# Three batch-1 projections with the weights as the moving operand, in four column tiles

## The chip, the cores and the metric

The program runs on one core of one Trainium2 chip. The metric is the time in device microseconds. One more execution was taken with the hardware profiler; its rows are what this document reads. Engines are named as the profile does: PE is TensorE's matmul, PEld its weight load, DVE is VectorE, ACT ScalarE, POOL GpSimd, SP the queue that issues the DMAs.

## The reference

Eight rows (batch 8, one token each, 448 wide) go through four layers: attention, a feed-forward layer, the same attention again, the same feed-forward again. The second attention reads the same cache with other queries.

```
W = min(4096, max(256, Sk // 4))                 # 1024 keys, the last of the cache
q = (layernorm(x) @ wq) -> 16 heads of 256       # 8 K/V heads, two query heads each
p = softmax(q k^T * 256 ** -0.5);  o = p v
x = x + o.reshape(4096) @ wo                     # wo: 4096 x 448
h = silu(layernorm(x) @ w1)                      # w1: 448 x 1792
x = x + h @ w2                                   # w2: 1792 x 448
```

Every batch row has its own K and V cache, 8 heads x 1024 x 256 of each in bf16: 16 tiles of 512 KB for a row. All weights stay in on-chip memory.

## The kernel before, in words

The first attention's queries (layer 0) are computed for all eight rows at the start, and the last feed-forward at the end for all eight rows at once. Between them the kernel goes row by row: `layer1(b)` is attention 0 of row b; `layer2(b)` is `chain(b)` (feed-forward, then the second attention's queries) followed by attention 1 of the same row on the same K and V tiles. Attention 0 of row b+1 is interleaved with attention 1 of row b, so one period holds both.

- **Slots.** 27 buffers hold K and V tiles. Tile number n is loaded when tile n-27 has been read for the last time (`pump`, L774), in one SP queue.
- **Attention.** VectorE transposes each K tile in place in two halves (L795, 16 per row). `scores` (L557) has the query block as stationary operand (8 columns) and 256 K columns moving, in four column tiles of TensorE (`tile_position=(0, 32*j)`), 64 matmuls for each half k2 of the heads. `softmax` (L564) takes the maximum of all scores, exponentiates on ScalarE, transposes on TensorE (L585). `pv_rows` (L616) multiplies by V, also in four column tiles with 256 moving columns; `pv_cols` (L645) does heads 4 to 7 of layer 0 the other way round.
- **Projections.** `proj` (L446, matmul on L453) holds a 128x128 (or 112x128) block of the weight as stationary operand and streams the activation column, repeated 32 times. `wo_part` adds `o @ wo` into bank XB, on top of x, which `x_init` (L675) put there; `w2` adds into the same bank. So the result stands as a column: 112 partitions x 4.
- **The chain of one row**, `chain(b)` (L685): copy x (L687, ACT), `stats1` (L657: sums on PE into bank STB, mean on DVE, Ln and Exp on ACT), `w1`, the silu steps (L693 to L701), `w2`, copy x again (L708), stats again, `wq` in two halves (L718) with the mean correction on DVE (L720), `q_blocks` (L536 on PE, L540 on DVE: the block-diagonal query `qbd`). The factor 1/std times 1/16 is applied later, inside the softmax (L577 and the scale of L580).

**What sets the order.** Every piece of work is a task with an engine, an assumed duration and the buffers it reads and writes; a bank of PSUM is one such buffer. `Plan.schedule` (L71) places the tasks by rank (longest remaining path), filling gaps, and the result is a fixed order for each engine; `Plan.emit` adds the semaphore waits. Two tasks on one bank keep the order in which the program adds them. Before, STB and the bank LB[1] of attention 1 are both bank 5, so `stats1` of row b+1 stands behind all of attention 1 of row b that touches bank 5.

The lines below are the few that set this up; the functions follow.

```
SC, OB, LB = [0, 1], [2, 3], [4, 5]
XB, YB, STB = 6, 7, 5
```

## Time and profile before

| | |
|---|---|
| median of 3 runs | 330.06 us (329.56 to 332.94) |
| the profiled execution | 331.38 us, of which its span is 329.6 us |
| busy: PE, PEld, DVE, ACT | 223.5, 166.3, 147.3, 50.7 us |
| chain that ended last, by engine | PE 48%, SP queue 18%, DVE 12%, ACT 9%, issue 8%, DMA 4% |
| costliest lines of that chain | projections L453 22%, L616 11%, L557 8% |
| mean granted clock of TensorE | 0.788 |
| moved by DMA | 78.51 MB, mean 238 GB/s |

How to read it: up to about 74 us the sixteen DMA engines never rest (weights and the first two rows' tiles); from 95 to 294 us stand six periods that repeat with the same order on every engine; the last 36 us hold the last row's chain, its attention 1 and the closing feed-forward for all rows. A period is counted here from one copy L687 to the next.

### The profile page before, as it was taken

How to read it: one execution, taken by the hardware profiler on the slowest of the kernel's cores; microseconds unless marked ns; L12 is line 12 of the kernel's file. 1: busy time of each engine (PE TensorE's matmuls, PEld its weight loads, DVE VectorE, ACT ScalarE, POOL GpSimd, SP SyncE). 2: the span in 40 equal slices, each digit the busy share in tenths (PEclk: the TensorE clock that was granted, in tenths of full speed). 3: DMA queues.
4: the chain of work that ended last, by engine and by line, in shares of the span. 5: the costliest groups of instructions: out<-in, count | busy, mean ns of one | idle time of the engine just before them, and what ended most of it. 6: DMA issues, size and time to landing. Idle time of an engine off the chain costs nothing.

```text
span 329.6 us, 13056 instructions
## 1 busy us (share of the span) xinstructions
PE 223.5 (68%) x6082; PEld 166.3 (50%) x6082; DVE 147.3 (45%) x426; ACT 50.7 (15%) x163; POOL 10.5 (3%) x22
## 2 busy tenths in 40 slices
...
GB/s 199 261 383 387 366 341 229 374 391 325 339 271 174 186 382 204 259 75 371 329 255 38 368 362 262 50 373 349 258 78 346 314 275 29 311 5 3 2 4 2
DMA packets 49991, 78.51 MB, mean 238 GB/s; under 512 B 2177, under 2 KB 40849, under 8 KB 49489
## 3 DMA queue, kind: packets, MB, share of 16 engines
...
q8 instruction: 47, 0.77, 0.9%
q14 instruction: 8, 0.06, 0.0%
HBM read 77.67 MB, written 0.01 MB: 236 GB/s over the span
## 4 chain that ended last, share of the span: by engine, by line
PE 48%; SPq 18%; DVE 12%; ACT 9%; issue 8%; DMA 4%; ACTq 0%
PE bank L453 22%; PE bank L616 11%; PE bank L557 8%; SPq L429 7%; SPq L417 7%; DVE slot L795 5%; DMA slot<-in_A_k_cache_dram 4%; ACT e_sb L580 4%; PE bank L645 3%; PE bank L585 2%; DVE mseg L566 2%; SPq L423 1%; DVE qbd L540 1%; ACT o_sb L623 1%; PE bank L625 1%
## 5 line engine op out<-in xcount | busy, mean ns | idle before, releaser
L795 DVE STREAM_TRANSPOSE slot<-slot 128x512 uint32<-128x512 uint32 x128 | 80.4, 681 | 14.2 <-DMA slot<-in_A_k_cache_dram 14.2
L557 PE MATMUL bank<-slot,qbd 128*8 128x256 bf16 x1024 | 50.8, 346 | 20.4 <-DVE slot L795 10.1
L616 PE MATMUL bank<-slot,pT_sb 128*2 128x256 bf16 x768 | 40.2, 330 | 11.7 <-DMA slot<-in_A_v_cache_dram 4.4
L557 PEld LDWEIGHTS bank<-slot,qbd 128*8 128x8 bf16 x1024 | 25.2, 98 | 34.5 <-DVE slot L795 11.4
L453 PE MATMUL bank<-oT,wo_sb 128*128 128x32 bf16 (+1 forms) x1152 | 38.0, 180 | 3.5 <-issue 2.9
L453 PEld LDWEIGHTS bank<-oT,wo_sb 128*128 128x128 bf16 x1152 | 33.9, 100 | 10.1 <-issue 5.1
L453 PE MATMUL bank<-xbt,wq_sb 112*128 112x32 bf16 x1024 | 32.6, 186 | 6.6 <-issue 4.5
L453 PEld LDWEIGHTS bank<-xbt,wq_sb 112*128 112x128 bf16 x1024 | 29.5, 103 | 12.2 <-issue 9.2
L651 DVE TENSOR_TENSOR oT<-bank,rl_sb 128x4 bf16<-128x4 f32 x32 | 5.2, 163 | 49.0 <-PE bank L645 48.7
L616 PEld LDWEIGHTS bank<-slot,pT_sb 128*2 128x2 bf16 x768 | 14.9, 87 | 19.2 <-issue 10.4
L453 PE MATMUL bank<-hT,w_sb 128*128 128x32 bf16 x448 | 13.3, 187 | 13.7 <-DVE hT L701 13.7
L645 PE MATMUL bank<-pT_sb,slot 128*128 128x2 bf16 x512 | 18.0, 164 | 5.5 <-issue 3.9
L453 PE MATMUL bank<-xbt,w_sb 112*128 112x32 bf16 (+1 forms) x504 | 17.4, 181 | 3.9 <-issue 3.4
L453 PEld LDWEIGHTS bank<-hT,w_sb 128*128 128x128 bf16 x448 | 12.5, 103 | 14.5 <-DVE hT L701 14.5
L645 PEld LDWEIGHTS bank<-pT_sb,slot 128*128 128x128 bf16 x512 | 15.6, 99 | 8.1 <-issue 6.3
L566 DVE TENSOR_REDUCE mseg<-bank 128x2 f32<-128x512 f32 x16 | 11.1, 692 | 17.9 <-PE bank L557 17.9
L580 ACT ACTIVATE e_sb<-bank,mb 128x256 bf16<-128x256 f32 x16 | 6.7, 470 | 75.2 <-DVE mb L573 75.2
L453 PEld LDWEIGHTS bank<-xbt,w_sb 112*128 112x128 bf16 x504 | 15.2, 101 | 4.4 <-issue 3.7
L525 POOL TENSOR_TENSOR qbd<-q1s,mask 128x256 bf16<-128x256 bf16 x16 | 9.8, 613 | 236.6 <-PE bank L557 211.6
L623 ACT ACTIVATE o_sb<-bank 128x256 bf16<-128x256 f32 x24 | 9.2, 383 | 48.9 <-PE bank L616 48.9
L598 DVE TENSOR_REDUCE l_sb<-bank 128x16 f32<-128x64 f32 x16 | 3.6, 225 | 24.7 <-PE bank L593 24.7
L629 DVE TENSOR_TENSOR oT<-bank,rl_sb 128x16 bf16<-128x16 f32 x24 | 5.1, 211 | 17.5 <-PE bank L625 16.7
...
## 6 DMA issues: line engine op xcount, KB each, us to landing
...
qbd<-in_A_x_dram SPq DMA_DIRECT2D x1, 7.0 KB
out_dram<-e_sb SPq DMA_DIRECT2D x1, 7.0 KB
```

The costliest lines, as they stand in the source:

```text
L417: dma(lambda e: e.dma_start(slots[s][:, :].rearrange("p (u d) -> p u d", d=DH), A_k_cache[b, kvh, S0:SK, :].rearrange("(p u) d -> p u d", ...
L429: dma(lambda e: e.dma_start(slots[s][:, :].rearrange("v (j n) -> v j n", j=4), src.rearrange("j (v uh) d -> v j (uh d)", uh=2)), [("slot", ...
L453: fns.append(lambda e, o=o, i=i: e.matmul(bank[bank_i][:, col + (o - outs[0]) * n:col + (o - outs[0] + 1) * n], lhs(o, i), rhs(i).broadcas ...
L525: add("pool", lambda e, k2=k2: e.tensor_tensor(qbd[0][:, 4 * k2:4 * k2 + 4, :, :].rearrange("p k c (q r) -> p (k c) q r", r=2), q1s[:, b, ...
L557: fns.append(lambda e, cb=cb, par=par, j=j, kvh=kvh, kv=kv: e.matmul(bank[sc][32 * j:32 * j + 8, k2 * 256:(k2 + 1) * 256], qbd[qi][:, kvh, ...
L566: dve(lambda e: e.tensor_reduce(mseg[ei][:, 0:2], bank[sc][:].rearrange("p (k n) -> p k n", k=2), AX.X, ALU.max, negate=True), bk(sc), [(" ...
L580: act(lambda e, k2=k2: e.activation(e_sb[ei][:, k2, :, :].rearrange("p uh (jj ul) -> p uh jj ul", ul=4), bank[sc][:, k2 * 256:(k2 + 1) * 2 ...
L585: pe([lambda e, c=c: e.matmul(bank[lb][:].bitcast(BF16)[:, c * P:(c + 1) * P], e_sb[ei][:, c // 2, c % 2, :], ident[:, :], is_transpose=Tr ...
L616: fns.append(lambda e, q=q, uh=uh, j=j, vv=vv: e.matmul(bank[ob][32 * j:32 * j + 2, k2 * DH:(k2 + 1) * DH], pT_sb[ei][:, k2 * 2 + uh, j * ...
L623: act(lambda e: e.activation(o_sb[oi][:], bank[ob][:, k2 * DH:(k2 + 1) * DH], ACTF.Copy), bk(ob), [("o", oi)], 0.42, prio, "oev")
L645: fns.append(lambda e, a=a, q=q, uh=uh: e.matmul(bank[vb][:, c0 + 2 * a:c0 + 2 * a + 2], vs[:, (2 * q + uh) * DH + a * P:(2 * q + uh) * DH ...
L795: dve(lambda e, v=v: e.transpose(v, v), [("slot", s)], [("slot", s)], 0.7, prio, "KT")
```

## The change

`wo`, `w2` and `wq` (the second attention's) swap operands: the activation column is the stationary operand (one column), and the weight rows are the moving one, 448 columns for `wo` and `w2` and 512 for `wq`. Four matmuls in turn go to the four column tiles, so four partial rows stand on partitions 0, 32, 64 and 96 of a bank.

- `wo` takes 32 matmuls for a row instead of 128, `w2` 14 instead of 56, `wq` 32 instead of 128.
- A new `fold`: ACT copies bank XB (448 columns, all partitions) to `rowb` in bf16, and four matmuls with a vector that is 1 on the four partitions add the partial rows into column form on top of x, which now stands in bank YB. It runs after `wo` and after `w2`, ahead of the copies of x.
- The query path: DVE makes the normalised `xn` (it needs 1/std, which the old order needed only in the softmax); `wq` half k2 gives four rows; ACT copies them to `rowb` (512 columns, with the factor 1/16), four matmuls turn them into columns, ACT copies these to `qT2`. Gone: the correction on DVE (L720), `rs16`, the rescaling of the maximum (L577) and the scale of L580.
- `stats1` now writes bank XB, not bank 5. `w1` keeps its form with 16 instead of 32 repeats. Banks XB and YB are zeroed at the start.

```diff
-    rs16 = [sb(f"rs16_{i}", [P, 1], F32) for i in range(2)]
+    rowb = sb("rowb", [P, 512], BF16)
+    ones4 = sb("ones4", [P, 1], BF16)
+    xn = sb("xn", [P, KC], BF16)
...
-    C_L, C_O, C_Q, C_ST = 256, 320, 352, 480
+    C_L, C_O, C_Q, C_ST, C_QT = 256, 320, 352, 480, 496
     C_XF = 256
-    CW = 32
+    C_W1 = 32
+    CW = 16
+    ONES4 = [("ones4", i) for i in range(5)]
 
...
-    for i in SC + OB:
+    for i in SC + OB + [XB, YB]:
...
-        if scale is not None:
-            act(lambda e: e.activation(mb[ei][:, 0:2], mb[ei][:, 0:2], ACTF.Copy, scale=scale[:, 0:1]),
-                [("mb", ei)] + scale_reads, [("mb", ei)], 0.2, prio)
         for k2 in range(2):
             act(lambda e, k2=k2: e.activation(
                 e_sb[ei][:, k2, :, :].rearrange("p uh (jj ul) -> p uh jj ul", ul=4),
                 bank[sc][:, k2 * 256:(k2 + 1) * 256].rearrange("p (ul uh jj) -> p uh jj ul", ul=4, uh=2),
-                ACTF.Exp, bias=mb[ei][:, k2:k2 + 1], scale=1.0 if scale is None else scale[:, 0:1]),
-                bk(sc) + [("mb", ei)] + scale_reads, [("e", ei, k2)], 0.5, prio, "exp")
+                ACTF.Exp, bias=mb[ei][:, k2:k2 + 1], scale=1.0),
+                bk(sc) + [("mb", ei)], [("e", ei, k2)], 0.5, prio, "exp")
         pe([lambda e, c=c: e.matmul(
...
-        s1, s2 = bank[STB][:, C_ST:C_ST + 1], bank[STB][:, C_ST + 1:C_ST + 2]
+        s1, s2 = bank[XB][:, 0:1], bank[XB][:, 1:2]
...
     def x_init(b, prio):
-        pe(lambda e: e.matmul(
-            bank[XB][:, 0:KC * CW], ident[0:CP, :], xb0[0:CP, :, b:b + 1].broadcast_to([CP, KC, CW]), start=True, stop=True),
-           ["ident", "xb0"], bk(XB), 0.08, prio, "xinit")
+        pe(lambda e: e.matmul(bank[YB][:, 0:KC], ident[0:CP, :], xb0[0:CP, :, b], start=True, stop=True),
+           ["ident", "xb0"], bk(YB), 0.05, prio, "xinit")
 
     def wo_part(b, kvhs, prio):
 
-        ins = [4 * kvh + i for kvh in kvhs for i in range(4)]
-        pe(proj(XB, 0, range(KC), ins, wo_l, lambda i: oT1[:, i % 2, i // 2:i // 2 + 1], 1, fresh=False),
-           [("oT1", 2 * kvh) for kvh in kvhs] + WO_R, bk(XB), 16 * MM * len(kvhs), prio, "wo")
+        fns = []
+        for kvh in kvhs:
+            for c in range(4):
+                i = 4 * kvh + c
+                fns.append(lambda e, i=i, c=c, kvh=kvh: e.matmul(
+                    bank[XB][32 * c:32 * c + 1, 0:D], oT1[:, i % 2, i // 2:i // 2 + 1], wo_sb[:, i * D:(i + 1) * D],
+                    start=(kvh == 0), stop=(kvh == HKV - 1), tile_position=(0, 32 * c), skip_group_check=True))
+        pe(fns, [("oT1", 2 * kvh) for kvh in kvhs] + WO_R, bk(XB), 0.24 * len(kvhs), prio, "wo")
+
+    def fold(prio):
+
+        act(lambda e: e.activation(rowb[:, 0:D], bank[XB][:, 0:D], ACTF.Copy), bk(XB), ["rowb"], 0.56, prio, "rowb")
+        pe([lambda e, c=c: e.matmul(bank[YB][0:CP, c:c + 1], rowb[:, c * CP:(c + 1) * CP], ones4[:, :],
+                                    start=False, stop=True, skip_group_check=True) for c in range(KC)],
+           ["rowb"] + ONES4, bk(YB), 0.13, prio, "fold")
 
     def chain(b, prio):
-        xp = bank[XB][0:CP, 0:KC * CW:CW]
-        act(lambda e: e.activation(xbt[0:CP, :], xp, ACTF.Copy), bk(XB), ["xbt"], 0.2, prio, "xb")
+        xp = bank[YB][0:CP, 0:KC]
+        fold(prio)
+        act(lambda e: e.activation(xbt[0:CP, :], xp, ACTF.Copy), bk(YB), ["xbt"], 0.2, prio, "xb")
         stats1(prio)
         for o0, o1 in ((0, 4), (4, 8), (8, 11), (11, 14)):
-            pe(proj(YB, o0 * CW, range(o0, o1), range(KC), w1_l, lambda i: xbt[0:CP, i:i + 1], 1),
-               ["xbt"] + W1_R, bk(YB), (o1 - o0) * KC * MM, prio + (0 if o0 == 0 else 0.1), "w1")
-        y1 = bank[YB][:, 0:FC * CW:CW]
+            pe(proj(YB, C_W1 + o0 * CW, range(o0, o1), range(KC), w1_l, lambda i: xbt[0:CP, i:i + 1], 1, fresh=False),
+               ["xbt"] + W1_R, bk(YB), (o1 - o0) * KC * MM, prio, "w1")
+        y1 = bank[YB][:, C_W1:C_W1 + FC * CW:CW]
         dve(lambda e: e.scalar_tensor_tensor(out=vneg[:], in0=ncs1[:], scalar=nmean[:, 0:1], in1=y1,
                                              op0=ALU.mult, op1=ALU.subtract),
-            bk(YB) + ["ncs1", "nmean"], ["vneg"], 0.23, prio + 0.2, "vneg")
+            bk(YB) + ["ncs1", "nmean"], ["vneg"], 0.23, prio, "vneg")
         act(lambda e: e.activation(den[:], vneg[:], ACTF.Exp, scale=rstd[:, 0:1]), ["vneg", "rstd"], ["den"], 0.31,
-            prio + 0.2, "silu")
-        act(lambda e: e.activation(den[:], den[:], ACTF.Copy, bias=-1.0, scale=-1.0), ["den"], ["den"],
-            0.2, prio + 0.2)
-        dve(lambda e: e.reciprocal(den[:], den[:]), ["den"], ["den"], 0.24, prio + 0.2)
+            prio, "silu")
+        act(lambda e: e.activation(den[:], den[:], ACTF.Copy, bias=-1.0, scale=-1.0), ["den"], ["den"], 0.2, prio,
+            "den")
+        dve(lambda e: e.reciprocal(den[:], den[:]), ["den"], ["den"], 0.24, prio, "rden")
         dve(lambda e: e.scalar_tensor_tensor(out=hT[:], in0=vneg[:], scalar=rstd[:, 0:1], in1=den[:],
                                              op0=ALU.mult, op1=ALU.mult),
-            ["vneg", "rstd", "den"], ["hT"], 0.23, prio + 0.2)
-        for h in range(2):
-            pe(proj(XB, 0, range(KC), range(7 * h, 7 * h + 7), w2_l, lambda i: hT[:, i:i + 1], 1, fresh=False),
-               ["hT"] + W2_R, bk(XB), 28 * MM, prio + 0.2, "w2")
-        prio += 0.3
-        act(lambda e: e.activation(xbt[0:CP, :], xp, ACTF.Copy), bk(XB), ["xbt"], 0.2, prio, "xb")
+            ["vneg", "rstd", "den"], ["hT"], 0.23, prio, "hT")
+        pe([lambda e, f=f: e.matmul(
+            bank[XB][32 * (f % 4):32 * (f % 4) + 1, 0:D], hT[:, f:f + 1], w2_sb[:, f * D:(f + 1) * D],
+            start=(f < 4), stop=(f >= FC - 4), tile_position=(0, 32 * (f % 4)), skip_group_check=True)
+            for f in range(FC)], ["hT"] + W2_R, bk(XB), 14 * 0.06, prio, "w2")
+        fold(prio)
+        act(lambda e: e.activation(xbt[0:CP, :], xp, ACTF.Copy), bk(YB), ["xbt"], 0.2, prio, "xb")
         stats1(prio)
-        act(lambda e: e.activation(x2s[0:CP, :, b], xp, ACTF.Copy), bk(XB), [("x2s", b)], 0.2, prio, "x2s")
-        dve(lambda e: e.tensor_scalar(rs16[b % 2][:], rstd[:], SCALE, None, op0=ALU.mult), ["rstd"],
-            [("rs16", b % 2)], 0.16, prio + 0.2)
+        act(lambda e: e.activation(x2s[0:CP, :, b], xp, ACTF.Copy), bk(YB), [("x2s", b)], 0.2, prio, "x2s")
+        dve(lambda e: e.tensor_scalar(xn[0:CP, :], xbt[0:CP, :], nmean[0:CP, 0:1], rstd[0:CP, 0:1],
+                                      op0=ALU.add, op1=ALU.mult), ["xbt", "nmean", "rstd"], ["xn"], 0.2, prio, "xn")
         for k2 in range(2):
-            wb = (YB, XB)[k2]
-            pr = prio + (0 if k2 == 0 else 0.3)
-            for p4 in range(4):
-                o0 = 16 * k2 + 4 * p4
-                pe(proj(wb, 4 * p4 * CW, range(o0, o0 + 4), range(KC), wq_l, lambda i: xbt[0:CP, i:i + 1], 1),
-                   ["xbt"] + WQ_R, bk(wb), 16 * MM, pr + (0 if o0 == 0 else 0.1), "wq")
-            dve(lambda e, k2=k2, wb=wb: e.scalar_tensor_tensor(
-                out=qT2[:, 16 * k2:16 * k2 + 16], in0=csq[:, 16 * k2:16 * k2 + 16], scalar=nmean[:, 0:1],
-                in1=bank[wb][:, 0:16 * CW:CW], op0=ALU.mult, op1=ALU.add),
-                bk(wb) + ["csq", "nmean"], [("qT2", k2)], 0.24, pr + 0.1, "qT2")
-            q_blocks(1, 1, k2, qT2[:, 16 * k2:16 * k2 + 16], [("qT2", k2)], pr + 0.15)
+            wb = (XB, YB)[k2]
+            pe([lambda e, j=j, c=c, k2=k2, wb=wb: e.matmul(
+                bank[wb][32 * j:32 * j + 1, :], xn[0:CP, c:c + 1],
+                wq_sb[0:CP, c, (4 * k2 + j) * 512:(4 * k2 + j + 1) * 512],
+                start=(c == 0), stop=(c == KC - 1), tile_position=(0, 32 * j), skip_group_check=True)
+                for c in range(KC) for j in range(4)], ["xn"] + WQ_R, bk(wb), 16 * 0.066, prio, "wq")
+            act(lambda e, wb=wb: e.activation(rowb[:], bank[wb][:], ACTF.Copy, scale=SCALE), bk(wb), ["rowb"], 0.62,
+                prio, "qrow")
+            lb = LB[1]
+            pe([lambda e, c=c, k2=k2: e.matmul(
+                bank[lb][:, C_QT + c:C_QT + 16:4], rowb[:, c * P:(c + 1) * P], ident[:, 0:P:32],
+                start=True, stop=True) for c in range(4)], ["rowb", "ident"], bk(lb), 0.12, prio, "qturn")
+            act(lambda e, k2=k2: e.activation(qT2[:, 16 * k2:16 * k2 + 16], bank[lb][:, C_QT:C_QT + 16], ACTF.Copy),
+                bk(lb), [("qT2", k2)], 0.2, prio, "qT2")
+            q_blocks(1, 1, k2, qT2[:, 16 * k2:16 * k2 + 16], [("qT2", k2)], prio)
...
```

The planner makes a new order of this. The names: `oT` is attention 0's output, `pT` the transposed probabilities, `xbt` x in bf16, `hT` the silu result, `qT` the query columns. First PE, from the last `wo` of a row to `w2` of its chain, before:

```order
L453 MATMUL bank<-oT,wo_sb 128x32 x16
L616 MATMUL bank<-slot,pT_sb 2x256 x16
L593 MATMUL bank<-pT_sb,ones_b 128x64 x2
L453 MATMUL bank<-oT,wo_sb 128x32 x16
L616 MATMUL bank<-slot,pT_sb 2x256 x8
L625 MATMUL bank<-ident,o_sb 128x8 x2
L453 MATMUL bank<-xbt,w_sb 128x32 x16
L625 MATMUL bank<-ident,o_sb 128x8 x2
L453 MATMUL bank<-xbt,w_sb 128x32 x16
L659 MATMUL bank<-xbt,ones_b 128x1 x4
L661 MATMUL bank<-xbt 128x1 x4
L453 MATMUL bank<-xbt,w_sb 128x32 x24
```

and the same place now, up to the second fold:

```order
L689 MATMUL bank<-wo_sb,oT 1x448 x16
L621 MATMUL bank<-slot,pT_sb 2x256 x16
L598 MATMUL bank<-pT_sb,ones_b 128x64 x2
L697 MATMUL bank<-ones,rowb 112x1 x4
L621 MATMUL bank<-slot,pT_sb 2x256 x8
L461 MATMUL bank<-xbt,w_sb 128x16 x32
L664 MATMUL bank<-xbt,ones_b 128x1 x4
L666 MATMUL bank<-xbt 128x1 x4
L461 MATMUL bank<-xbt,w_sb 128x16 x24
L621 MATMUL bank<-slot,pT_sb 2x256 x8
L630 MATMUL bank<-ident,o_sb 128x8 x2
L721 MATMUL bank<-w_sb,hT 1x448 x14
```

Before, all 64 products with V of attention 1 (L616 on bank 3) stand ahead of L659, 56 of them ahead of the last `wo`. Now none of them stands ahead of the last `wo`, and all 64 (L621) stand in the chain behind it, up to just before `wq`.

Second PE, from the second stats of the chain into the scores, before:

```order
L453 MATMUL bank<-xbt,wq_sb 128x32 x48
L659 MATMUL bank<-xbt,ones_b 128x1 x4
L661 MATMUL bank<-xbt 128x1 x4
L453 MATMUL bank<-xbt,wq_sb 128x32 x16
L557 MATMUL bank<-slot,qbd 8x256 x8
L536 MATMUL bank<-qT,sel 128x8x2 x4
L557 MATMUL bank<-slot,qbd 8x256 x48
```

and now:

```order
L664 MATMUL bank<-xbt,ones_b 128x1 x4
L666 MATMUL bank<-xbt 128x1 x4
L621 MATMUL bank<-slot,pT_sb 2x256 x8
L733 MATMUL bank<-wq_sb,xn 1x512 x16
L630 MATMUL bank<-ident,o_sb 128x8 x2
L741 MATMUL bank<-ident,rowb 128x4 x4
L544 MATMUL bank<-qT,sel 128x8x2 x4
L565 MATMUL bank<-slot,qbd 8x256 x56
L733 MATMUL bank<-wq_sb,xn 1x512 x16
L565 MATMUL bank<-slot,qbd 8x256 x8
L741 MATMUL bank<-ident,rowb 128x4 x4
```

Before, `wq` runs ahead of the statistics; now it stands behind them. Of the 56 scores 24 are attention 0's and 32 attention 1's first half. Third DVE, at the same place now (`xn`, a K transpose, attention 1's output, a K transpose, the query block, the last eight K transposes):

```order
L729 TENSOR_SCALAR xn<-xbt,nmean,rstd 112x4
L817 STREAM_TRANSPOSE slot<-slot 128x512
L634 TENSOR_TENSOR oT<-bank,rl_sb 128x2x8
L817 STREAM_TRANSPOSE slot<-slot 128x512
L548 TENSOR_TENSOR qbd<-bank,mask 128x256
L817 STREAM_TRANSPOSE slot<-slot 128x512 x8
L548 TENSOR_TENSOR qbd<-bank,mask 128x256
```

The eight transposes stand behind the first query block now as before (there L540, L795 x8). PE has 4,337 matmuls in all where it had 6,081; a period has 481 where it had 699.

## Rows read from the trace of the kernel before

**Rows 1.** Windows: us, busy and count of PE, PEld, DVE, ACT, POOL; PEclk, DMA share, GB/s.

```profile
229.60:264.50 34.90, 26.04 (x703) 18.71 (x699) 16.90 (x48) 5.80 (x19) 1.23 (x2) 0.74 0.72 245
264.50:293.75 29.25, 24.61 (x703) 18.36 (x699) 15.14 (x45) 5.80 (x19) 0.00 (x0) 0.82 0.51 165
293.75:329.60 35.85, 24.33 (x672) 19.11 (x664) 9.06 (x35) 6.31 (x22) 0.00 (x0) 0.62 0.01 3
```

**Rows 2.** Timeline of ACT: start, us, line, operation; in brackets idle time before it.

```profile
94.90 0.17 ACT L687 ACTIVATE xbt<-bank 112x4 bf16<-112x4 f32 x1 [4.83 <-PE bank L453]
...
270.50 0.17 ACT L708 ACTIVATE xbt<-bank 112x4 bf16<-112x4 f32 x1 [2.31 <-PE bank L453]
...
293.75 0.17 ACT L687 ACTIVATE xbt<-bank 112x4 bf16<-112x4 f32 x1 [3.20 <-PE bank L453]
```

**Rows 3.** Timeline of all engines in the period that begins at 264.50.

```profile
264.98 0.55 PE L453 MATMUL bank<-xbt,w_sb 112*128 112x32 bf16 x16
...
266.05 0.25 PE L659 MATMUL bank<-xbt,ones_b 112*128 112x1 bf16 x4
...
266.44 0.16 DVE L664 TENSOR_SCALAR nmean<-bank 128x1 f32<-128x1 f32 x1 [0.45 <-PE bank L661]
...
267.25 0.29 ACT L671 ACTIVATE rstd<-lnv,hlnd_sb 128x1 f32<-128x1 f32 x1
...
268.78 1.68 PE L453 MATMUL bank<-hT,w_sb 128*128 128x32 bf16 x56 [1.76 <-DVE hT L701]
...
273.33 0.25 PE L536 MATMUL bank<-qT,sel 128*128 128x16 bf16 x4
...
273.62 0.42 DVE L540 TENSOR_TENSOR qbd<-bank,mask 128x256 bf16<-128x256 f32 x1 [0.52 <-PE bank L536]
...
273.96 4.85 DVE L795 STREAM_TRANSPOSE slot<-slot 128x512 uint32<-128x512 uint32 x8
...
277.08 1.02 PE L557 MATMUL bank<-slot,qbd 128*8 128x256 bf16 x16
...
279.37 1.09 PE L557 MATMUL bank<-slot,qbd 128*8 128x256 bf16 x32
...
280.53 0.69 DVE L566 TENSOR_REDUCE mseg<-bank 128x2 f32<-128x512 f32 x1 [0.75 <-PE bank L557]
...
283.93 1.04 PE L616 MATMUL bank<-slot,pT_sb 128*2 128x256 bf16 x32 [0.46 <-ACT pT_sb L589]
...
285.59 0.54 PE L645 MATMUL bank<-pT_sb,slot 128*128 128x2 bf16 x16
...
286.61 0.95 PE L453 MATMUL bank<-oT,wo_sb 128*128 128x32 bf16 x32
```

**Rows 4.** Groups of instructions by line: busy us, mean ns of one, idle before.

```profile
L515 ACT ACTIVATE q1s<-bank 128x512 bf16<-128x512 f32 x1 | 0.6, 597 | 19.2 <-PE bank L507 19.2
L623 ACT ACTIVATE o_sb<-bank 128x256 bf16<-128x256 f32 x24 | 9.2, 383 | 48.9 <-PE bank L616 48.9
```

**Rows 5.** The page: busy times, then the instruction queue (packets, MB, share).

```profile
PE 223.5 (68%) x6082; PEld 166.3 (50%) x6082; DVE 147.3 (45%) x426; ACT 50.7 (15%) x163; POOL 10.5 (3%) x22
...
q8 instruction: 47, 0.77, 0.9%
```

**Rows 6.** Timeline of PE: first and last of 14 gaps put down to "issue".

```profile
97.49 0.21 PE L453 MATMUL bank<-xbt,w_sb 112*128 112x32 bf16 x2 [1.56 <-issue]
...
274.74 1.87 PE L557 MATMUL bank<-slot,qbd 128*8 128x256 bf16 x30 [0.27 <-issue]
```

**Rows 7.** Windows of one microsecond, PE alone: busy (count), granted clock, DMA, GB/s.

```profile
277.00:278.00 1.00, 1.00 (x22) 0.50 0.00 0
...
296.00:297.00 1.00, 0.07 (x3) 1.00 0.06 16
...
299.00:300.00 1.00, 0.73 (x27) 0.50 0.00 0
```

**Rows 8.** Timeline of PE: attention 0's last scores of row 1.

```profile
77.03 1.85 PE L557 MATMUL bank<-slot,qbd 128*8 128x256 bf16 x32 [2.43 <-DVE slot L795]
```

30 lines of the change are left out of this document (17 added, 13 removed).

## The prediction

> **What bounds the kernel now.** I read the windows by period first, then the timeline of one period, then the gaps of TensorE, then its clock. From one copy L687 to the next the kernel repeats: 94.90 to 293.75 are six periods [rows 2], 33.14 us each, and PE is busy 24.6 to 26.0 us of one [rows 1]. DMA is busy 0.72 of a period of 34.90 us, 25.1 us [rows 1]. So no engine fills the period; what fills it is one ring of waits: chain of row b, last scores of row b+1, softmax, `wo` of row b+1, next chain. I cut the period 264.50 to 293.75, which has almost no gap, into four stretches [rows 1 to 3]:
> A, copy of x to second copy of x: 270.50 - 264.50 = 6.00.
> B, to the maximum of attention 0's scores: 280.53 - 270.50 = 10.03.
> C, to the first `wo`: 286.61 - 280.53 = 6.08.
> D, to the next copy of x: 293.75 - 286.61 = 7.14.
> Together 29.25. The mean period is 3.9 longer, and 2.96 of that are gaps in which PE waits for nothing that the profile shows: 14 of them between 94.90 and 293.75, 17.76 us in all [rows 6]. The page has 47 packets of the instruction queue, 0.77 MB; PE issues 6,082 matmuls and 6,082 loads, about 259 for each packet [rows 5]. I take the gaps for PE waiting for its next piece of program.
>
> **Prices.** A column-tiled matmul with 256 columns costs 1.04 us / 32 = 33 ns where the clock is full (2.4 GHz) and 1.02 / 16 = 64 ns where it is half (1.2 GHz) [rows 3, 7]. Nothing in the trace streams 448 or 512 columns in tiles. The lower end is the same 33 and 64, as if columns were free; the upper end is twice the proportional price. I take the proportional one, since the time halves with the clock, as work on columns would: 57 and 112 ns for 448, 65 and 128 for 512. The old form costs 1.68 / 56 = 30 ns at half clock [rows 3]. So `wo` goes from 3.8 us to 1.8 (full) or 3.6 (half), `w2` from 1.7 to 0.8 or 1.6, `wq` from 3.8 to 2.1 or 4.1: at half clock nothing is won on PE.
>
> The Trainium skill, "TensorE: Matmul & The Clock Gate", section "Part 3: Packing small matmuls", gives a pack of tiles one matmul's latency plus about 4 ns for each further tile; by its latency formula that is an estimate of 71 ns a matmul for four tiles of 256 columns, if packs do not overlap. The 33 ns of the trace contradict that, so the row decides. By the Trainium skill (91 and 98 ns) the three projections would cost about 2.7 us more per period than by my full-clock price.
>
> **A.** New: ACT copies 448 columns, 0.54 us (between 0.383 for 256 and 0.597 for 512 [rows 4]), then four small matmuls to the next engine's start, 0.29 (273.33 to 273.62), the copy of x 0.17, and two handovers of 0.05 [rows 2, 3]: `w1` starts 1.10 after the last `wo` where it started 264.98 - 264.50 = 0.48 after it. The small output matmuls that stood between `w1` pieces move out, about -0.1. So +0.5; at half clock the 16 products with V that now stand ahead of the fold last 1.02 and cover more than the copy, +1.0. `w2` with what follows: 1.72 before (268.78 to 270.50); now 0.80 + 0.05 + 0.54 + 0.05 + 0.29 + 0.05 = 1.78, at half clock 1.57 + 1.02 + 0.34 = 2.93. A becomes 6.6 (full) or 8.2 (half). The 64 products with V, 2.1 to 4.1 us of PE, lie here beside the waits for ACT and DVE.
>
> **B.** Before, `wq` ran while the statistics were made; now it waits for them: copy and handover 0.22, sums to mean 0.39 (266.05 to 266.44), mean to 1/std 1.10 (to 267.54), `xn` about 0.16 like the mean, two handovers: 1.97. `wq`'s first half 16 x 65 ns = 1.04 (2.05), ACT copy of 512 columns 0.60, four matmuls 0.29, copy 0.17, four matmuls 0.29, three handovers: 4.51 (5.52). The query block 0.42: ready at 4.93 (5.94) after the copy of x, before at 3.54 (274.04). Behind it DVE still has eight K transposes, 4.85 [rows 3]; the last scores of attention 0 start at 9.8 where they started at 8.87. At half clock PE is later than DVE: 32 + 16 scores 3.07, `wq`'s second half 2.05, and then a second round of copy, turn, copy, select 1.5, which stands ahead of those scores in PE's order: 12.6. Scores to maximum 1.16. B becomes 11.0 (full), 13.7 (half), or 12.7 with only `wq`'s first half at full clock.
>
> **C.** The query product L540 no longer stands among the steps of the maximum; its price of 0.42 is the upper end, zero the lower, I take 0.25. The rescaling and the second exponential no longer end last ahead of `wo`; `wo` follows the first V columns: 3.40 - 0.25 + 1.66 + 0.54 = 5.35.
>
> **D.** Left are 32 x 57 ns and three groups of V columns of 0.54 [rows 3]: 3.45 (full), 5.2 (half); 7.14 before.
>
> **Elsewhere.** ACT gains 2.3 us a period on 5.8 [rows 1]: cover enough, its order lets nothing early wait behind a late copy. POOL and SP keep their order. DVE's new memsets lie ahead of the first K tiles' arrival. V tiles are issued behind attention 1's scores; the first half's 32 end at 4.93 + 1.06 = 6.0 after the second copy of x, and the products that need those tiles start at 11.0 + 3.15 = 14.2: 8 us of cover, and if it is gone, the next thing late is L621 waiting for DMA. The 47 pieces of program become 34 (4,337 x 2 / 259); gaps by the same ratio, 2.96 x 481 / 699 = 2.0 a period; ends 1.0 and 2.96.
>
> **The clock.** It fell to half in stretches with pauses (296.00 to 297.00 PE is 7% busy, from 299.00 the clock is 0.50) and rose after PE had run on without a pause: at 277.00 it is 0.50 with PE busy throughout, and the scores at 279.37 run at the full price [rows 3, 7]. Stretch C ran at full clock here (33 ns), B mostly at half (64 ns). New stretch D is one unbroken run; new B has five us with little work on PE, then an unbroken run of scores. So I take C full, D nearly so, A in the middle, B half from the scores on: 7.2 + 12.7 + 5.35 + 3.9 = 29.15, with gaps 31.2, against 33.14: -1.95, six times, -11.7.
>
> **Start and end.** 77.03 to 94.90 [rows 2, 8], 17.87 us, is scores, C and D of row 1: now 1.9 + 5.35 + 3.9 + a gap of 1.0 = 12.1, and about 1 later because of the longer query path: -4.8. The data that come before do not change. The last stretch, 35.85 us at a mean clock of 0.62 [rows 1], gets A's 1.2 and about 1.6 of B, less 0.3 for the rescaling: +2.5. Sum: -11.7 - 4.8 + 2.5 = -14.0 on the profiled execution's 331.4, so 317.4. The median of the runs is 1.3 lower than that execution, so I forecast **316**.
>
> **Rivals.**
> (1) *The clock stays at half in the chain.* The change puts more handovers between small pieces into A and B. All half but C: 8.2 + 13.7 + 5.35 + 5.2 = 32.45, with gaps 34.5: +1.35 six times, start -3.5, end +4: 339, slower. It decides from 31.5 a period without gaps, 70% of the way from my middle to all half. For it: the clock of the last two periods is 0.74 and 0.82 [rows 1]. Against: D loses every pause. The Trainium skill, "TensorE: Matmul & The Clock Gate", section "Loop structure matters more than you think", says that pauses between bursts of matmuls throttle the clock; the rows of 296 to 299 agree.
> (2) *The clock is mostly full and gaps shrink to 1.0.* 26.4 + 1.0 = 27.4: -34, start -5.8, end +1: 291. Below 25.1 DMA would bound, so not much further. For it: streaming weights keep PE at work.
> (3) *Column tiles of 448 columns cost twice as much.* +0.8 in A, +1.0 in B, +1.8 in D, 3.6 a period: 338.
> (4) *The gains are given back:* V products delay the chain at half clock and gaps stay at 2.96: 316 + 5.5 + 6 = 327.
>
> **Chances.** Forecast 0.56 (its own range 306 to 329), (1) 0.14, (2) 0.18, (3) 0.04, (4) 0.08. One per cent, what a measurement here can tell from no change, is 3.3 us. Faster: 0.52 of the forecast's, all of (2), 0.02 of (4): 0.72. Within 1%: 0.04 and 0.06: 0.10. Slower 0.18. Range 299 to 335: it leaves out half of (2) and the larger part of (1) and (3).
>
> **What would show it.** In the profile after: `wo` at 57 ns a matmul, full clock; D of 3.5 to 4; the L621 products inside the chain; the query block 5 to 6 us after the second copy of x (if at 4, the path was overpriced); the last scores behind the eighth transpose (DVE) or behind the second turn (PE). It is wrong if A grows by more than 2 us, if a K transpose waits for DMA, or if the gaps do not fall with the program's length.

## The result, and the profile after

The changed kernel takes 315.81 us (median of 4 runs, 313.53 to 317.09) against 329.81 us for the kernel before (median of 4, 327.59 to 332.94); the ratio is 0.959, with a 95% interval of 0.9505 to 0.9674. The profiled execution is the fastest of the four, 313.53 us with a span of 311.7. The forecast was 316. Ratios here and below leave out executions that lie more than 1.5% above the fastest of their kernel, and three profiles (wq old with 16 columns, changed + fill, w2 old + fill) are of such executions, so that their stretches are only a guide.

The page of the changed kernel first: the line of busy times and that of the instruction queue, which answer to [rows 5].

```profile
PE 217.1 (70%) x4338; PEld 125.9 (40%) x4338; DVE 147.3 (47%) x418; ACT 66.4 (21%) x203; POOL 10.5 (3%) x22
q8 instruction: 34, 0.56, 0.7%
```

The program is 34 packets long, as the prediction reckoned from 47. Now its windows (columns: stretch, its length, busy time of PE, PEld, DVE, ACT and POOL, granted clock, DMA share, GB/s): the six periods, from the first ACT copy after row 1's last `wo` to the same copy of row 7, and the last stretch.

```profile
87.29:270.00 182.71, 145.51 (x2896) 82.95 (x2892) 100.11 (x270) 46.49 (x144) 6.12 (x10) 0.73 0.80 269
270.00:311.70 41.70, 29.78 (x608) 18.01 (x596) 9.09 (x34) 8.54 (x28) 0.00 (x0) 0.55 0.01 2
```

Against [rows 1] and [rows 2]: a period is 182.71 / 6 = 30.45 us where it was 33.14; the last stretch is 41.70 where it was 35.85; what lies ahead of the first period ends at 87.29 and not at 94.90. Together -16.14 + 5.85 - 7.61 = -17.90 us of span. ACT is busy 46.49 / 6 = 7.75 us a period, 1.95 more than before; 2.3 more were forecast. Two gaps of TensorE are left in the whole span, 1.03 us together, where there were 14 in the periods alone [rows 6].

The timeline of TensorE in one period, at the end of the chain and behind it (start, length, engine, line, operation, how many, and what ended an idle time before it); `...` marks rows left out:

```profile
178.78 0.37 PE L697 MATMUL bank<-ones,rowb 128*112 128x1 bf16 x4
182.94 1.65 PE L721 MATMUL bank<-w_sb,hT 128*1 128x448 bf16 x14
184.02 1.43 PE L621 MATMUL bank<-slot,pT_sb 128*2 128x256 bf16 x16
185.38 0.53 PE L697 MATMUL bank<-ones,rowb 128*112 128x1 bf16 x4
185.84 0.59 PE L621 MATMUL bank<-slot,pT_sb 128*2 128x256 bf16 x8
...
188.25 1.87 PE L733 MATMUL bank<-wq_sb,xn 112*1 112x512 bf16 x16 [0.99 <-DVE xn L729]
190.05 0.21 PE L630 MATMUL bank<-ident,o_sb 128*128 128x8 bf16 x2
190.83 0.27 PE L741 MATMUL bank<-ident,rowb 128*128 128x4 bf16 x4 [0.56 <-ACT rowb L738]
191.38 0.28 PE L544 MATMUL bank<-qT,sel 128*128 128x16 bf16 x4 [0.28 <-ACT qT L744]
...
206.54 0.95 PE L650 MATMUL bank<-pT_sb,slot 128*128 128x2 bf16 x32
207.42 1.40 PE L689 MATMUL bank<-wo_sb,oT 128*1 128x448 bf16 x16
208.48 0.79 PE L621 MATMUL bank<-slot,pT_sb 128*2 128x256 bf16 x16
```

ACT's copies in it, which mark the stretches:

```profile
178.18 0.54 ACT L696 ACTIVATE rowb<-bank 128x448 bf16<-128x448 f32 x1 [4.85 <-PE bank L689]
184.64 0.54 ACT L696 ACTIVATE rowb<-bank 128x448 bf16<-128x448 f32 x1 [2.02 <-PE bank L621]
185.95 0.17 ACT L726 ACTIVATE xbt<-bank 112x4 bf16<-112x4 f32 x1 [0.77 <-PE bank L697]
```

A is 7.77 us here. Behind the last `wo` stand 16 products with V (L621), behind `w2` 16 and behind the second fold 8, in the time in which the chain waits for ACT and DVE; [rows 3] has none there from `w1` to the scores. From `w2` to the second copy of x it is 3.01 us, where it was 1.72. The clock in the four pieces that follow:

```profile
182.00:186.00 4.00, 3.27 (x40) 1.77 (x44) 2.45 (x6) 1.18 (x5) 0.00 (x0) 0.50 0.90 296
186.00:190.00 4.00, 3.01 (x40) 0.76 (x32) 1.28 (x4) 1.02 (x5) 0.00 (x0) 0.50 0.49 153
190.00:194.00 4.00, 3.16 (x58) 1.79 (x58) 3.10 (x7) 0.78 (x2) 0.00 (x0) 0.50 0.98 334
194.00:198.00 4.00, 3.28 (x73) 1.72 (x65) 3.29 (x6) 0.78 (x2) 0.61 (x1) 0.83 0.73 238
```

From `w2` through the first scores the granted clock is 0.50, 1.2 GHz. So the new forms run at both levels, which gives their prices; the rows at the higher one:

```profile
164.74 1.03 PE L733 MATMUL bank<-wq_sb,xn 112*1 112x512 bf16 x16
165.60 0.41 PE L565 MATMUL bank<-slot,qbd 128*8 128x256 bf16 x8
...
177.20 0.93 PE L689 MATMUL bank<-wo_sb,oT 128*1 128x448 bf16 x16
177.96 0.61 PE L621 MATMUL bank<-slot,pT_sb 128*2 128x256 bf16 x16
```

From the start of one row to the start of the next, a matmul of `wq` costs 0.86 / 16 = 54 ns at full clock and 1.80 / 16 = 112 at half, one of `wo` 0.76 / 16 = 47 at full clock.

### The profile page after: what moved, and what is told of

Its sections match the earlier page's. It is cut to its first block, busy times and chain, and to the rows that moved or that the text cites. A ratio compares the mean times of both kernels' runs of the same rounds, so it can differ in the third digit from the quotient of the medians.

```text
span 311.7 us, 9602 instructions
## 1 busy us (share of the span) xinstructions
PE 217.1 (70%) x4338; PEld 125.9 (40%) x4338; DVE 147.3 (47%) x418; ACT 66.4 (21%) x203; POOL 10.5 (3%) x22
## 4 chain that ended last, share of the span: by engine, by line
PE 54%; SPq 13%; ACT 12%; DVE 10%; DMA 7%; issue 4%; ACTq 0%
PE bank L621 10%; PE bank L565 10%; SPq L437 7%; PE bank L733 7%; PE bank L461 5%; DMA w_sb<-in_B_w_dram 5%; PE bank L689 5%; PE bank L721 4%; PE bank L650 4%; ACT rowb L738 3%; DMA slot<-in_A_v_cache_dram 2%; DVE slot L817 2%; SPq L425 2%; PE bank L697 2%; ACT e_sb L585 2%
## 5 line engine op out<-in xcount | busy, mean ns | idle before, releaser
L621 PE MATMUL bank<-slot,pT_sb 128*2 128x256 bf16 x768 | 45.5, 352 | 8.8 <-DMA slot<-in_A_v_cache_dram 4.8
L733 PE MATMUL bank<-wq_sb,xn 112*1 112x512 bf16 x256 | 25.6, 540 | 8.9 <-DVE xn L729 8.9
L621 PEld LDWEIGHTS bank<-slot,pT_sb 128*2 128x2 bf16 x768 | 19.8, 95 | 19.7 <-issue 9.8
L689 PE MATMUL bank<-wo_sb,oT 128*1 128x448 bf16 x256 | 21.2, 430 | 0.4 <-DVE oT L656 0.3
L585 ACT ACTIVATE e_sb<-bank,mb 128x256 bf16<-128x256 f32 x32 | 13.4, 472 | 37.2 <-DVE mb L581 37.2
L696 ACT ACTIVATE rowb<-bank 128x448 bf16<-128x448 f32 x16 | 8.7, 544 | 54.2 <-PE bank L689 37.9
L738 ACT ACTIVATE rowb<-bank 128x512 bf16<-128x512 f32 x16 | 9.5, 597 | 48.1 <-PE bank L733 48.1
L650 PEld LDWEIGHTS bank<-pT_sb,slot 128*128 128x128 bf16 x512 | 15.0, 99 | 11.9 <-issue 6.3
L590 PE MATMUL bank<-ident,e_sb 128*128 128x128 bf16 x64 | 7.6, 254 | 15.2 <-ACT e_sb L585 15.2
L461 PE MATMUL bank<-xbt,w_sb 112*128 112x16 bf16 (+1 forms) x504 | 15.6, 170 | 0.8 <-issue 0.5
L461 PEld LDWEIGHTS bank<-xbt,w_sb 112*128 112x128 bf16 x504 | 14.2, 99 | 2.9 <-ACT xbt L704 1.8
L733 PEld LDWEIGHTS bank<-wq_sb,xn 112*1 112x1 bf16 x256 | 6.5, 104 | 21.1 <-DVE xn L729 12.2
L574 DVE TENSOR_REDUCE mseg<-bank 128x2 f32<-128x512 f32 x16 | 10.8, 673 | 8.9 <-PE bank L565 8.9
```

Of the source, the lines that this page charges most:

```text
L461: fns.append(lambda e, o=o, i=i: e.matmul(bank[bank_i][:, col + (o - outs[0]) * n:col + (o - outs[0] + 1) * n], lhs(o, i), rhs(i).broadcas ...
L574: dve(lambda e: e.tensor_reduce(mseg[ei][:, 0:2], bank[sc][:].rearrange("p (k n) -> p k n", k=2), AX.X, ALU.max, negate=True), bk(sc), [(" ...
L585: act(lambda e, k2=k2: e.activation(e_sb[ei][:, k2, :, :].rearrange("p uh (jj ul) -> p uh jj ul", ul=4), bank[sc][:, k2 * 256:(k2 + 1) * 2 ...
L621: fns.append(lambda e, q=q, uh=uh, j=j, vv=vv: e.matmul(bank[ob][32 * j:32 * j + 2, k2 * DH:(k2 + 1) * DH], pT_sb[ei][:, k2 * 2 + uh, j * ...
L650: fns.append(lambda e, a=a, q=q, uh=uh: e.matmul(bank[vb][:, c0 + 2 * a:c0 + 2 * a + 2], vs[:, (2 * q + uh) * DH + a * P:(2 * q + uh) * DH ...
L689: fns.append(lambda e, i=i, c=c, kvh=kvh: e.matmul(bank[XB][32 * c:32 * c + 1, 0:D], oT1[:, i % 2, i // 2:i // 2 + 1], wo_sb[:, i * D:(i + ...
```

## The experiments

The table holds every run that bears on the sum. A is from ACT's first copy after the last `wo` to the second copy of x; the next column goes from there to the first `wo`; D from there to the next first copy. All are means over the six periods, in us, read from the timelines as above, gaps included; "gaps" is TensorE's idle time without a releaser. Each ratio is to runs of the kernel before that were taken together with that experiment; their medians lie between 329.0 and 329.8 us. "Old forms" are weight-stationary, "sums moved" means out of bank 5, and a "fill" is explained at its experiment.

| kernel | A | to `wo` | D | gaps | period | last stretch | median | ratio to before |
|---|---|---|---|---|---|---|---|---|
| before | 6.63 | 16.63 | 9.88 | 2.96 | 33.14 | 35.85 | 329.8 | 1 |
| old forms, sums moved | 7.71 | 17.86 | 6.58 | 1.62 | 32.14 | 35.52 | 322.8 | 0.9858 [0.9795, 0.9921] |
| new forms, sums not moved | 8.71 | 18.11 | 6.21 | 0.47 | 33.03 | 40.73 | 336.2 | 1.0233 [1.0154, 1.0313] |
| changed kernel | 8.18 | 18.26 | 4.01 | 0.17 | 30.45 | 41.70 | 315.8 | 0.959 [0.9505, 0.9674] |
| w2 old | 6.81 | 18.68 | 3.64 | 0.11 | 29.13 | 36.81 | 301.8 | 0.9199 [0.9119, 0.928] |
| wq old, 16 columns | 8.95 | 17.29 | 4.41 | 0.04 | 30.65 | 37.46 | 311.3 | – |
| wq old, 32 columns | 8.98 | 16.62 | 4.21 | 0.96 | 29.82 | 36.91 | 308.1 | 0.9368 [0.9287, 0.9449] |
| both old, w2 in halves | 8.59 | 18.51 | 4.66 | 0.96 | 31.75 | 38.96 | 315.5 | 0.9625 [0.9559, 0.9691] |
| both old, w2 whole | 7.78 | 18.26 | 4.31 | 1.09 | 30.35 | 37.50 | 310.3 | 0.9404 [0.9311, 0.9497] |
| changed + fill | 7.85 | 17.38 | 4.66 | 0.00 | 29.89 | 37.75 | 302.2 | 0.9095 [0.9001, 0.9188] |
| w2 old + fill | 7.35 | 18.77 | 4.87 | 0.33 | 30.98 | 37.67 | 309.2 | 0.9357 [0.9284, 0.9429] |
| w2 old + 3 fills | 7.28 | 19.51 | 3.87 | 0.95 | 30.66 | 36.85 | 313.9 | 0.9477 [0.9392, 0.9563] |
| before + fill | 6.79 | 16.68 | 9.55 | 2.78 | 33.03 | 34.80 | 332.3 | 1.0106 [1.0065, 1.0147] |

**The bank alone.** The diff also moves the sums of the row statistics out of bank 5. Here only that is done, to the kernel before:

```diff
-        s1, s2 = bank[STB][:, C_ST:C_ST + 1], bank[STB][:, C_ST + 1:C_ST + 2]
+        s1, s2 = bank[LB[0]][:, C_ST:C_ST + 1], bank[LB[0]][:, C_ST + 1:C_ST + 2]
...
```

> The kernel before with one change: the sums of the row statistics stand in bank 4, no longer in bank 5, so the products with V of the second attention need no longer stand ahead of the statistics; the projections keep their old form (6,081 matmuls). Theory 'form' (the gain comes from the projections: fewer, longer matmuls in the stretch from the first wo on, and fewer pieces of program): the 14 gaps of TensorE stay, 2.5 to 3.2 us a period, the stretch from the first wo to the next copy of x falls from 7.1 us by at most 1.5, and the time is 322 to 332 us. Rival 'order' (the moved bank alone does it): that stretch falls to about 4.5 us, and the time is 314 to 319 us, like the changed kernel's.

Measured: 322.84 us. The V products do go into the chain, as these rows of TensorE show, and delay `w2`, whose halves now stand 1.8 us apart:

```profile
226.95 0.93 PE L453 MATMUL bank<-hT,w_sb 128*128 128x32 bf16 x28 [0.55 <-DVE hT L701]
227.81 1.02 PE L616 MATMUL bank<-slot,pT_sb 128*2 128x256 bf16 x16
228.76 0.93 PE L453 MATMUL bank<-hT,w_sb 128*128 128x32 bf16 x28
229.62 1.02 PE L616 MATMUL bank<-slot,pT_sb 128*2 128x256 bf16 x16
```

D falls by 3.3 us (0.8 of it gaps), A and the way to `wo` grow by 2.3. The time lies in the range of "form", but D fell by more than "form" allowed and the gaps shrank. The bank alone gives 1.4% of the 4.1%, about a third, so neither theory is whole.

**The forms alone.** The changed kernel, its sums back in bank 5:

```diff
-        s1, s2 = bank[XB][:, 0:1], bank[XB][:, 1:2]
+        s1, s2 = bank[STB][:, C_ST:C_ST + 1], bank[STB][:, C_ST + 1:C_ST + 2]
...
```

> The changed kernel with the statistics' sums back in bank 5, where the second attention's columns are: the other half of the first experiment, the new projections with the old rule for the V products (4,337 matmuls). Theory 'program' (what the periods gain is the gaps of TensorE that shorter program leaves out): gaps stay under 0.5 us a period, the stretches only trade with each other (from the first wo to the next copy longer by 1 to 2 us, to the second copy of x shorter by as much), and the time is 312 to 319 us. Rival 'order' (V products in the chain's waits are what gains): 321 to 327 us.

Measured: 336.15 us, slower than before and beyond both theories. TensorE between the first `wo` and the chain, and then in it:

```profile
187.57 0.96 PE L689 MATMUL bank<-wo_sb,oT 128*1 128x448 bf16 x8
188.32 0.64 PE L621 MATMUL bank<-slot,pT_sb 128*2 128x256 bf16 x8
188.89 0.58 PE L650 MATMUL bank<-pT_sb,slot 128*128 128x2 bf16 x16
189.41 0.59 PE L621 MATMUL bank<-slot,pT_sb 128*2 128x256 bf16 x8
189.93 0.58 PE L650 MATMUL bank<-pT_sb,slot 128*128 128x2 bf16 x16
190.44 1.29 PE L689 MATMUL bank<-wo_sb,oT 128*1 128x448 bf16 x12
...
198.51 1.66 PE L721 MATMUL bank<-w_sb,hT 128*1 128x448 bf16 x14 [1.77 <-DVE hT L718]
200.80 0.54 PE L697 MATMUL bank<-ones,rowb 128*112 128x1 bf16 x4 [0.63 <-ACT rowb L696]
...
203.49 1.87 PE L733 MATMUL bank<-wq_sb,xn 112*1 112x512 bf16 x16 [1.51 <-DVE xn L729]
```

The products with V stand ahead of `wo` and of the chain again, and the chain, now longer by its copies, has nothing beside it: 1.77, 0.63 and 1.51 us of idle TensorE in one chain. Its six periods have a clock of 0.69, those of the changed kernel 0.73. So by the ratios the bank is worth 1.4% with the old forms and 6.4% with the new, and the forms cost 2.3% without it and gain 2.7% with it. The intervals of the two crossed kernels exclude 1 but lie partly within 2% of it. The gaps stay away (0.47 a period), and it is slow all the same: fewer gaps alone do not make the time, and the theory "program" falls.

**One projection put back at a time.** First `w2` alone, with the one moving column that the old form needs, straight into the columns of x:

```diff
...
-            for f in range(FC)], ["hT"] + W2_R, bk(XB), 14 * 0.06, prio, "w2")
-        fold(prio)
...
+            pe([lambda e, o=o, i=i: e.matmul(bank[YB][:, o:o + 1], w2_l(o, i), hT[:, i:i + 1],
+                                             start=False, stop=True, skip_group_check=True)
...
```

> The changed kernel with w2 alone in the old form, 56 matmuls with one moving column each straight into the columns that hold x, so that the second copy of 448 columns and the second fold fall away; 4,641 matmuls. Theory 'two losses': from the start of w2 to the second copy of x 1.7 us and not 3.0, so 1.3 us a period, seven times 9 us: 305 to 309 us. Rival 'cover': the second copy of x comes 1.3 us earlier but the last scores still wait for the K transposes or the query path's second half: 312 to 317 us. Rival 'program': at 304 matmuls more the gaps take back 0.5 us a period: 309 to 312 us.

Measured: 301.81 us, a larger gain than any of the three expected, and a version that beats both kernels. Its `w2`, the row behind it, and its windows over the periods and the last stretch:

```profile
179.37 1.62 PE L722 MATMUL bank<-hT,w_sb 128*128 128x1 bf16 x56
180.92 0.59 PE L621 MATMUL bank<-slot,pT_sb 128*2 128x256 bf16 x8
```

```profile
87.03:261.79 174.76, 141.06 (x3124) 86.70 (x3115) 100.54 (x270) 43.81 (x138) 6.12 (x10) 0.77 0.84 282
261.79:298.60 36.81, 25.52 (x646) 17.34 (x634) 9.07 (x34) 8.10 (x27) 0.00 (x0) 0.69 0.01 2
```

56 small matmuls take 1.55 us, and the second copy of x comes 1.68 us after their start, not 2.99: A shrinks by 1.37 as expected. The 4.9 us of the last stretch were not expected; its clock is 0.69 where the changed kernel has 0.55. In the kernel before, 56 matmuls of the old `w2` take 1.68 us and 32 of the old `wo` 0.95 [rows 3], 30 ns each, though the clock is 0.50 under the first and 1.00 under the second:

```profile
269.00:270.00 1.00, 1.00 (x44) 0.50 1.09 377
286.00:288.00 2.00, 1.76 (x57) 1.00 0.72 228
```

So at half clock the old form lost nothing there, where a column tile's price doubled (54 to 112 ns).

Then the query projection alone, with the old correction and the scale in the softmax; first with 16 moving columns, then with the 32 of the kernel before (the lines are of the second):

```diff
...
+                pe(proj(wb, 4 * p4 * 32, range(o0, o0 + 4), range(KC), wq_l, lambda i: xbt[0:CP, i:i + 1], 1, CW=32),
+                   ["xbt"] + WQ_R, bk(wb), 16 * MM, prio, "wq")
...
```

> The changed kernel with the query projection alone in the old form (128 weight-stationary matmuls that need not wait for the statistics, the correction on DVE, the scale in the second softmax); 5,041 matmuls. Theory 'two losses': the query block is ready 3.6 us after the second copy of x and not 6.0, the last scores wait for the eighth K transpose, the stretch to the maximum falls from 12.5 to 10.2 us, and the rescaling in the softmax gives 0.3 back: 2.0 us a period, with 0 to 1 us more of gaps: 301 to 311 us. Rival 'cover': 312 to 318 us. Rival 'program': gaps of 2 us or more a period and 313 us or more.

> The kernel with the old query projection once more, its moving operand now 32 columns wide as in the kernel before, where that experiment had 16 (5,041 matmuls, the same order). Theory 'columns' (the narrower matmuls let the clock fall): the mean clock rises from 0.756 to 0.78 or more and the time falls to 302 to 307 us. Rival 'no matter': clock within 0.02 and 308 to 313 us.

Measured: 311.32 us (304.64 to 312.27) and 308.06. The query block is ready 3.6 us after the second copy of x, and the last K transpose ahead of the scores ends at 9.0 where it ended at 10.8; but the second query block comes at 11.6 to 11.9 us in these two as in the changed kernel, and the scores behind it end last. The stretch to `wo` gains 1.0 to 1.6 us, not 2. The first time lies between the ranges of "two losses" and "cover", the second at the low end of "no matter". The runs of the two widths overlap (304.64 to 312.27 and 306.36 to 310.78): the width was not shown to matter.

Last both, so that `wo` alone is new, with `w2` in two pieces and in one:

> The changed kernel with w2 and wq back in the old form (weights stationary, the old query path and its scale in the softmax); wo stays in column tiles with one fold; 5,345 matmuls. Theory 'two losses' (column tiles pay in wo, and the copy, fold and turn that w2 and wq need cost more than they save): the stretch to the second copy of x falls from 8.0 to about 6.5 us, that to the maximum from 12.5 to about 10.2, the other two stay at 5.5 and 3.9, 26.1 together; with the gaps of TensorE between 0.2 and 2.0 a period, 26.3 to 28.1 against 30.45: 290 to 302 us. Rival 'cover' (the longer path of w2 and wq lies beside work of DVE and PE that ends last anyway): 313 to 319 us. Rival 'program' (the gaps come back with the matmuls and take the gain): 304 to 312 us, with gaps of 2.5 us or more a period.

> wo alone in the new form once more, with w2's 56 matmuls as one piece (in the second experiment 16 products with V stood between its halves) and the query projection's moving operand 32 columns wide. By the stretches of other runs: 6.8 to the second copy of x as with w2 old, 16.6 to the first wo and 4.2 behind it as with wq old, 27.6, with gaps of 0.5 to 1.0 a period 28.1 to 28.6 against 29.1 with w2 old alone: 293 to 300 us. Rival 'order' (the planner places the V products anew, and they delay w2 or the query path): 306 to 316 us.

Measured: 315.52 us, in the range of "cover", and 310.33, in that of "order"; the sum of the single gains (-14, -8) does not come. In the first, as in the rows of the bank alone, 16 products with V stand between the halves of `w2`:

```profile
216.08 0.90 PE L725 MATMUL bank<-hT,w_sb 128*128 128x1 bf16 x28 [0.55 <-DVE hT L721]
216.91 1.02 PE L624 MATMUL bank<-slot,pT_sb 128*2 128x256 bf16 x16
217.86 0.90 PE L725 MATMUL bank<-hT,w_sb 128*128 128x1 bf16 x28
```

The second mends that (1.69 us from `w2` to the copy), but its second query block comes at 13.6 us. So the order of the work, which the planner makes anew in each kernel, costs as much as the edit gives; which place in it costs how much was not taken apart.

**The program's length.** The changed kernel with waits that are long satisfied, ahead of the matmuls of the projections, until it is as long as the kernel before:

```diff
...
+                        for _ in range(PAD.get(t.name, 0) if e == "pe" else 0):
+                            eng.wait_ge(handles["x"], 16)
```

`PAD` is 12 for `wo` and `w2` and 11 for `wq`, 7,232 waits in all; in the traces stand 13,098 instructions against 9,602, so they take 3,496 of them, about two waits each.

> The changed kernel with 3,496 instructions more for TensorE's sequencer that compute nothing: waits, long since satisfied, on the first transfer's semaphore, 5 or 6 ahead of every matmul of wo, w2 and wq. Its program is as long as that of the kernel before (12,242 instructions against 12,228), its matmuls, data and order are those of the changed kernel. Theory 'program': the instruction queue shows 47 packets, gaps of over 1 us come back in the stretches from wo to w2, 2 to 3 us a period, and the time is 327 to 337 us. Rival 'shape' (the gaps belonged to the many small matmuls with their weight loads): at most what the waits themselves cost, under 0.7 us a period without gaps of over 1 us: 315 to 321 us.

Measured: 647.59 us, beyond both. One half of `wq`, and the queue:

```profile
306.48 9.22 PE L736 MATMUL bank<-wq_sb,xn 112*1 112x512 bf16 x16 [0.98 <-DVE xn L732]
315.63 0.21 PE L633 MATMUL bank<-ident,o_sb 128*128 128x8 bf16 x2
```

```profile
q8 instruction: 48, 0.79, 0.5%
```

The 16 matmuls take 9.15 us and not 1.80: the waits themselves cost, (647.59 - 315.81) / 3,496 = 95 ns for each instruction on the mean. So this tells nothing of the gaps, and the theory stays untested. What the other runs show: with 34 to 36 packets the gaps in the periods are 0 to 2.8 us in all, with 47 and 48 they are 9.7 to 17.8; but three kernels of equal length, 39 packets (the two with wq old, and w2 old with 3 fills), have 0.2, 5.7 and 5.7. Length goes with the gaps and does not fix them; that they are program fetches was not shown.

**Filling the pauses.** The changed kernel with matmuls that nobody reads, into a bank that is free during the chain:

```diff
...
+        pe([lambda e, i=i: e.matmul(bank[SC[1]][32 * (i % 4):32 * (i % 4) + 1, 0:D], ones_b[:, 0:1],
+                                    wo_sb[:, i * D:(i + 1) * D], start=True, stop=True, tile_position=(0, 32 * (i % 4)))
+            for i in range(n)], reads + ["ones_b"] + WO_R, bk(SC[1]), n * 0.05, prio, "fill")
...
+        fill(16, ["xbt"], prio + 0.5)
...
```

> The changed kernel with 32 matmuls more per row, column tiles of 448 columns whose results nobody reads: 16 in the wait for the hidden layer behind w1, 16 in the wait for xn ahead of wq, about 0.8 us of TensorE each at full clock (1.7 at half). Theory 'clock' (the half clock from w2 to the first scores is caused by these two pauses and costs 2 us a period or more): the clock from the second copy of x to the scores rises from 0.50 to 0.8 or more, and the time falls to 299 to 308 us. Rival 'busy' (the clock stays as it is, and the fillers stand in the way): 319 to 327 us. Between them, 312 to 319 us, the pauses do not set the clock or it gives no time.

Measured: 302.24 us (297.64 to 309.84), the second version that beats both kernels. In its four runs time goes with the mean clock: 309.84 us at 0.795, 303.49 at 0.881, 301.00 at 0.885, 297.64 at 0.903; the changed kernel's four had 0.751 to 0.781. The order of the other work is that of the changed kernel on TensorE and ACT, but for two small matmuls a row (L630, with their DVE step), so the gain is not one of a new order. The mean clock does not always tell the time: both old with w2 in halves took 315.30 us at 0.691 and 315.52 at 0.811. The window behind the fillers, in the profile of the slowest of them:

```profile
186.00:190.00 4.00, 3.50 (x72) 1.59 (x64) 2.07 (x6) 1.50 (x6) 0.00 (x0) 1.00 0.73 249
190.00:194.00 4.00, 2.97 (x62) 1.79 (x62) 3.24 (x7) 0.78 (x2) 0.00 (x0) 0.75 0.97 334
```

Where the changed kernel had 0.50 the clock is now 1.00 and 0.75. The Trainium skill, "TensorE: Matmul & The Clock Gate", section "Loop structure matters more than you think", says that pauses between bursts throttle the clock; these rows agree. Then the same in the version with `w2` old, with a third filler in the softmax, and in the kernel before:

> The kernel with w2 in the old form, with fillers as in the experiment before: 16 in the wait for the hidden layer, 8 in the wait for xn. Theory 'two costs' (the second copy and fold cost path, the pauses cost clock, and the two add): the 14 us that each saved by itself add to 284 to 294 us. Rival 'one cost' (w2 in the old form had already removed the pause that let the clock fall; its mean clock was 0.818): 297 to 305 us.

> That kernel with 16 fillers more per row in the wait of the first softmax, ahead of the products with V. Theory 'clock': the products with V and wo behind the softmax, which cost 64 and 106 ns in the periods where the clock had fallen, cost 33 and 48 throughout: about 1 us a period less than without this filler, 5 to 8 us in all. Rival 'busy': the fillers stand in front of scores or of the transpose of the exponentials: 0 to 6 us more than without.

> The kernel before, nothing of the change, with 16 fillers per row in the wait for the hidden layer. Theory 'clock' as a cost of either kernel: the scores of the stretch after the second copy of x run at full clock more often, and the time is 316 to 325 us. Rival 'new' (only the changed kernel has pauses long enough): 326 to 334 us.

Measured: 309.18 us, beyond both theories, 313.85, in the range of "busy", and 332.27, in that of "new"; all are slower than without the added fillers (by 7, 5 and 3 us). The clock rose in the last two (0.79 to 0.84 with three fillers, against 0.78 to 0.82 for `w2` old without; 0.80 to 0.85 in the kernel before, against 0.76 to 0.80), and the time rose all the same, so the work added cost more than it gave; with `w2` old and two fillers it hardly did (0.76 to 0.83). Here too the order on TensorE is otherwise the same, but for L630 in the first. So one fill gained, three did not; why stays open.

## Why the prediction came out right

Its total was right and its mechanism mostly, but with errors that cancel: on the profiled execution the periods gave 4.44 us more than forecast, the start 2.81 more and the end 3.35 less, 3.9 in all, and the median lies 2.3 above that execution, where the forecast put it 1.3 below. That the median came within 0.2 us is luck.

- **D: right.** 3.9 forecast, 4.01 measured; it was 9.88 with gaps, 7.14 in the period without [rows 1 to 3]. The products with V went into the chain, as said.
- **A: mis-sized, the half-clock figure.** The working gave 6.6 at full and 8.2 at half clock and took 7.2; measured 8.18. From `w2` to the copy of x: 2.93 forecast for half, 2.99 measured.
- **B and C: right.** 12.7 + 5.35 = 18.05 forecast, 12.47 + 5.79 = 18.26 measured. The first query block is ready at 6.07 us (5.94 forecast for half clock), and the last scores stand behind the second turn on TensorE, not behind the eighth transpose, as the forecast had it for half clock.
- **Gaps: mis-sized.** The step "gaps by the same ratio" gave 2.0 us a period, against 0.17: 11 us too many over six periods. The four stretches without gaps were 1.1 a period too short (29.15 against 30.28), which takes 6.8 of it back.
- **Start and end: mis-sized, both in the direction given.** -7.6 where -4.8 was forecast; +5.85 where +2.5 was, at a clock of 0.55 in place of 0.62. The start's last scores begin at 77.06 us, as before [rows 8]:

```profile
77.06 2.07 PE L565 MATMUL bank<-slot,qbd 128*8 128x256 bf16 x64 [1.10 <-DVE slot L817]
...
83.50 0.55 PE L689 MATMUL bank<-wo_sb,oT 128*1 128x448 bf16 x8
```

From there to the first `wo` it is 6.44 us, where 1.9 + 5.35 and 1 for the longer query path had been put, and from `wo` to the copy at 87.29 it is 3.79 without a gap, where 3.9 and a gap of 1.0 had been.

- **Prices.** 47 and 54 ns at full clock where the proportional price gave 57 and 65: between the ends, nearer to it than to the flat 33. At half clock 112 ns against the 128 of the forecast. By the Trainium skill, "TensorE: Matmul & The Clock Gate", section "Part 3: Packing small matmuls", the estimate was 91 and 98 ns; no row at full clock agrees. By these figures the estimate for the three projections is 2.6 us a period above the prediction's own price, not 2.7.
- **What the prediction did not separate.** It put the moved V products and the new forms into one sum. The runs show that the forms alone lose 2.3%, the bank alone gains 1.4%, and together they gain 4.1%: the column tiles put ACT copies and small matmuls into the chain, and the freed V products fill the waits that this makes. `w1` with 16 repeats in place of 32 is in every version with new forms and was not tried by itself.
- **The rivals.** (1) The half clock held from `w2` to the first scores, as "at half clock nothing is won on PE" feared, but not throughout: 0.73 over the periods, 0.74 before. (2) Gaps under 1.0, yes; a clock mostly full, no; the filled kernel's 297.64 us at 0.903 is near the 291 that it gave. (3) No. (4) The V products did delay the chain at half clock, but the gaps did not stay. Of the marks set for failure one came, by the working's own start: A grew by 2.18 against the 6.00 of the period that it cut, by 1.55 against the mean of six, so A is where the forecast was weakest. K transposes waited for DMA for 1.1 us in the six periods, as before (9.4 and 14.2 in the whole span), and the gaps fell by more than the program's length did.
